# Which weight tiles are prepared ahead, and half of a stage's gates on GpSimd, in a top-k attention with two MLPs

## The chip, the cores and the metric

The kernel runs on one core of a Trainium2 chip. The metric is device microseconds of one execution, the median of several runs. The engines are named as the profile names them: PE (TensorE), DVE (VectorE), ACT (ScalarE), POOL (GpSimd), and SP, whose queue issues all transfers.

## The reference

Attention over q, k, v of 4 batches, 8 heads, 576 positions and 64 features, in which only the 32 largest scores of each row count; its output is 2304 tokens of 512 features. Two MLPs follow, each 512 to 2048 to 512:

```python
scores = scale * np.matmul(q, k.transpose(0, 1, 3, 2))
kth = np.partition(scores, -top_k, axis=-1)[..., -top_k:-top_k + 1]
attn = softmax(np.where(scores >= kth, scores, -1e9))      # top_k = 32
x = (attn @ v) as 2304 x 512
h = x @ w_in;  x = (h - np.tanh(h)) @ w_out                # first MLP
h = x @ w2_in; out = np.where(h > 0, h, np.exp(np.minimum(h, 0)) - 1) @ w2_out
```

## The kernel before

The 2304 tokens are worked on in six chunks of 384. A chunk's attention has four pairs of heads and eight groups (two per pair), each of three tiles of 128 query rows by 576 keys. For a tile, PE makes the scores (`ps`), ACT copies them to SBUF (`s`, line 385), and DVE finds the 32 largest: four times MAX8 (line 406) with three MATCH_REPLACE8 between (line 420). ACT or DVE makes the masked exponential (`e`), PE transposes it (`pt`), ACT copies that (`ph`), PE multiplies by v (`av`), and the result, times the reciprocal of the sum, is the chunk's `x`. The scores of groups 16 to 23 are computed early, in the time of the first chunk's attention, and parked in DRAM (`park`, lines 347 to 356).

A chunk's two MLPs (m = 0 and 1) go through 16 f-tiles of 128 hidden features each, numbered 0 to 31 over both. A step multiplies `x` with an f-tile's first matrix (`first`, line 577, 12 matmuls into PSUM tile `h`), forms the gate (`gate`), and multiplies with the second matrix into three PSUM banks (`second`, line 613, 9 matmuls). `first` and `gate` of the next step are issued ahead of `second` of this one. Products are done in three terms, of a high and a low part of each operand: ACT rounds to the high part and POOL subtracts it (`split`, lines 147 to 149). The gate of the first MLP is h - tanh(h): ACT makes the tanh (`t`, line 580), and DVE subtracts (line 596). In chunks where `GATE_GP` is k, the f-tiles with ft % 4 < k have ACT copy h to SBUF (line 593) and POOL subtract (line 594) instead. The gate of the second MLP is on ACT and DVE (lines 582, 583 and 591).

The weights come as raw 8-byte words. `prepare` (lines 177 to 213) loads one f-tile's raw words (1 MB, line 180), scales and converts them on ACT (lines 186 and 203), joins them on DVE (line 189), splits them on ACT and POOL into a tile of the ring `w` of six slots, and stores that to DRAM (line 213) for the later chunks, which load it from there (line 222). While the attention of the first chunk still goes on, scaling and joining are done in two halves through PSUM banks; the switch `wide` ends that when the last pair of the first chunk is transposed (line 445). The first chunk's MLPs use the prepared tile itself; but the f-tiles in `EARLY` are prepared in advance, from tick `PREP_AT` on and `PREP_RATE` ticks apart, only stored, and loaded later like those of other chunks (`load_next`, lines 215 to 222).

The order of the code is by ticks, four to a group. The first MLP of the first chunk begins at tick 36; six ticks before, `load_next` is called for f-tiles 0 to 5, one each tick, and then once behind each step's `second`, six f-tiles ahead. The last pair of the first chunk is handled at tick 32, behind that tick's `load_next`. This order is a priority: the framework's scheduler fixes each engine's own order when it builds the program, by these priorities, by which buffers are free, and by a timeline that it models. In the trace the first raw words are loaded at 7.6 us. Lines touched: 47 and 51.

Of the kernel before, what the change touches and what calls it, by code (L numbers as in the profile page):

```python
# [43 lines left out]

MASK_ACT = [3, 2, 1, 0, 0, 0]

GATE_GP = [0, 0, 1, 1, 1, 2]

EARLY = range(12, 21)
PREP_AT = 8
PREP_RATE = 2.5
AHEAD = 6
# [52 lines left out]
def tile_topk_attention_two_mlps(  # L107
# [64 lines left out]
    def weight_tile(name):  # L172
        return sb.tile([P, 2, 2, 512], F32R, tag="w", name=name, bufs=W2_BUFS)
# [3 lines left out]
    def prepare(m, ft):  # L177

        raw = sb.tile([P, 1024], I64, tag="wr", name=f"wr{m}_{ft}", bufs=RAW_BUFS)
        nc.sync.dma_start(raw, (w1, w2)[m][ft])  # L180
        words = raw.bitcast(F32).rearrange("p (n w) -> p n w", w=2)
        low, scaled = words.bitcast(U32)[:, :, 0], words[:, :, 1]
        w = sb.tile([P, 1024], F32, tag="wf", name=f"wf{m}_{ft}", bufs=WF_BUFS)

        def scale(out, src):
            nc.scalar.activation(out, src, AF.Prelu, scale=2.0**-112, alpha=-(2.0**32))  # L186

        def join(out, high, low):
            nc.vector.scalar_tensor_tensor(  # L189
                out.bitcast(U32), high.bitcast(U32), 3, low, op0=ALU.logical_shift_left, op1=ALU.bitwise_or  # L190
            )

        halves = [slice(0, 512), slice(512, 1024)]
        small = {}
        early = "wide" in stage
        if early:
            for a, cs in enumerate(halves):
                small[a] = bank(f"acc{stage['at'] % 3}", f"sc{m}_{ft}_{a}", 1)
                stage["at"] += 1
                scale(small[a], scaled[:, cs])  # L200
        else:
            scale(scaled, scaled)
        nc.scalar.activation(low.bitcast(I32), low, copy, scale=2.0**-29 * (1 - 2.0**-20), bias=-0.5 + 7.5 * 2.0**-20)
        if early:
            for a, cs in enumerate(halves):
                join(w[:, cs], small[a], low[:, cs])
        else:
            join(w, scaled, low)
        wt = weight_tile(f"wp{m}_{ft}")
        if m * NF + ft not in EARLY:  # L210
            weights[0, m, ft] = wt
        split(wt[:, :, 0], wt[:, :, 1], w.rearrange("p (h c) -> p h c", h=2))
        nc.sync.dma_start(f(scratch[m, ft]), f(wt))

    def load_next():
        if loads:
            ci, m, ft = loads.pop(0)
            if ci == 0 and m * NF + ft not in EARLY:
                prepare(m, ft)
# [366 lines left out]
    def gate(ci, m, ft):  # L586
# [3 lines left out]
        if m == 1:  # L590
            nc.vector.scalar_tensor_tensor(g, t, -1.0, h, op0=ALU.add, op1=ALU.max)  # L591
        elif ft % 4 < GATE_GP[ci]:
            nc.scalar.activation(g, h, copy)
# [135 lines left out]

    early = list(EARLY)  # L730
    for tick in range(FIRST_TICK, n_ticks):
        for do in before.get(tick, ()):
            do()
        while early and PREP_AT + PREP_RATE * (len(EARLY) - len(early)) <= tick:
            i = early.pop(0)
# [77 lines left out]
```

## Time and profile before

| | |
|---|---|
| median of 3 runs | 1222.76 us (1219.91 to 1224.75) |
| the profiled execution | 1219.57 us, span 1217.8 us |
| busy: PE, DVE, ACT, POOL | 1146.4, 944.5, 765.6, 497.9 us |
| mean granted clock of PE | 0.973 of full speed |
| raw weight loads (`wr`) | 32 of 1024 KB |
| stores of prepared tiles (`w<-wp`) | 32 of 1024 KB |
| loads of prepared tiles (`wt<-w`) | 169 of 1024 KB |

Busy times are sums over the whole span; the ends of matmuls are modelled, so PE's share is not a share of its peak. In the row of slices each digit is the busy share of one of 40 equal slices of 30.4 us, in tenths. A view of stages gives each engine's busy time between two times; a timeline gives single instructions, merged where alike; what stands in brackets behind one is how long its engine had been idle, and what ended that. A group `out<-in` names the tiles that an instruction writes and reads; `f32<-128x576` and the like are shapes.

### The profile page before, as it was taken

Reading aid. Unit: us, or ns where it says so; the run is one execution under the profiler, and the core shown is the slowest. Engines: PE = TensorE matmul, PEld = TensorE weight load, DVE = VectorE, ACT = ScalarE, POOL = GpSimd, SP = SyncE. Lnnn points to the kernel's source line nnn. Section 1 sums busy time; section 2 is a strip of 40 time slices with the busy share of each in tenths; the row PEclk is TensorE's granted clock in tenths of the full one; section 3 lists DMA queues with packets and bytes.
Section 4 is the critical chain, followed back from the end, with each engine's and each line's share of the span. In section 5 each row is a group of like instructions: output and inputs, shape, how many; then the busy total and the mean of one; then the engine's idle time right before and its main releaser. Section 6 shows DMA issues by size and latency. Waiting matters only on the chain.

```text
span 1217.8 us, 18856 instructions
## 1 busy us (share of the span) xinstructions
PE 1146.4 (94%) x6349; PEld 977.0 (80%) x6349; DVE 944.5 (78%) x1898; ACT 765.6 (63%) x1594; POOL 497.9 (41%) x557
## 2 busy tenths in 40 slices
PE   6577689999999999999999999999999999999998
PEld 3344368888888979898978988988998888898887
DVE  7999999998999999679987789898889995100111
ACT  5999987888984555565664566575655564432333
POOL 2445446657753313443423444444334422333222
PEclk9688889999999999999999999999999999999999
DMA  7999937985979986669986779978688645686572
GB/s 246 398 333 330 311 111 276 350 266 217 356 285 327 276 294 184 238 166 299 241 182 234 242 204 260 251 219 266 225 241 243 204 127 207 210 283 248 198 269 95
DMA packets 81616, 301.69 MB, mean 248 GB/s; under 512 B 18800, under 2 KB 36080, under 8 KB 51696
## 3 DMA queue, kind: packets, MB, share of 16 engines
q1 hardware_dynamic: 81520, 300.49, 76.5%
q8 instruction: 50, 0.82, 0.3%
q14 instruction: 46, 0.38, 0.1%
HBM read 255.07 MB, written 45.39 MB: 247 GB/s over the span
## 4 chain that ended last, share of the span: by engine, by line
PE 75%; ACT 6%; DVE 5%; DMA 3%; issue 1%; POOL 1%; another core or an unknown queue 0%; ACTq 0%; DVEq 0%; POOLq 0%
PE h L577 30%; PE acc L613 30%; PE av L470 6%; PE pt L448 5%; DMA wt<-w 3%; PE ps L383 2%; PE ps L384 2%; DVE vm L406 2%; DVE w L420 2%; DVE wf L189 1%; ACT ph L449 1%; ACT s L385 1%; ACT e L410 1%; ACT y L627 1%; ACT wr L186 0%
## 5 line engine op out<-in xcount | busy, mean ns | idle before, releaser
L149 POOL TENSOR_TENSOR gl<-g,gh 128x384 fp32r<-128x384 f32 x192 | 205.3, 1071 | 385.0 <-ACT gh L148 360.2
L406 DVE MAX8 vm<-w 128x8 f32<-128x576 f32 x432 | 315.0, 748 | 3.1
L613 PE MATMUL acc<-wt,gh 128*128 128x512 f32 x1014 | 270.9, 398 | 0.3 <-ACT gh L148 0.3
L613 PEld LDWEIGHTS acc<-wt,gh 128*128 128x128 f32 x1014 | 186.2, 188 | 34.9 <-issue 3.3
L420 DVE MATCH_REPLACE8 w<-vm,w 128x576 f32<-128x576 f32 x288 | 212.7, 740 | 0.0
L148 ACT ACTIVATE gh<-g 128x384 fp32r<-128x384 f32 x192 | 100.7, 525 | 81.2 <-DVE g L591 34.6
L613 PE MATMUL acc<-wt,gl 128*128 128x512 f32 x507 | 148.9, 398 | 1.0 <-POOL gl L149 1.0
L577 PE MATMUL h<-zh,wt 128*128 128x384 f32 (+2 forms) x776 | 146.4, 324 | 2.4 <-ACT zh L632 2.0
L591 DVE SCALAR_TENSOR_TENSOR g<-t,h 128x384 f32<-128x384 f32 x96 | 52.2, 544 | 124.2 <-ACT t L583 123.8
L406 DVE MAX8 vm<-s 128x8 f32<-128x576 f32 x144 | 107.2, 750 | 47.1 <-ACT s L385 44.4
L577 PE MATMUL h<-xh,wt 128*128 128x384 f32 x672 | 140.9, 339 | 1.2 <-DMA wt<-w 1.2
L385 ACT ACTIVATE s<-ps 128x288 f32<-128x288 f32 (+1 forms) x272 | 107.5, 418 | 48.3 <-PE ps L384 40.7
L449 ACT ACTIVATE ph<-pt 116x384 f32<-116x384 f32 (+1 forms) x240 | 111.5, 499 | 40.0 <-PE pt L448 37.4
L448 PE MATMUL pt<-ident,e 128*116 128x128 f32 (+1 forms) x720 | 115.2, 288 | 22.7 <-ACT e L423 9.9
L577 PEld LDWEIGHTS h<-zh,wt 128*128 128x128 f32 x776 | 125.8, 189 | 8.8 <-ACT zh L632 3.2
L448 PEld LDWEIGHTS pt<-ident,e 128*116 128x116 f32 (+1 forms) x720 | 90.0, 142 | 43.2 <-ACT e L423 12.6
L577 PEld LDWEIGHTS h<-xh,wt 128*128 128x128 f32 x672 | 117.4, 188 | 7.5 <-ACT t L580 1.0
L582 ACT ACTIVATE t<-h 128x384 f32<-128x384 f32 x96 | 46.8, 489 | 119.7 <-PE h L577 119.7
L613 PEld LDWEIGHTS acc<-wt,gl 128*128 128x128 f32 x507 | 93.3, 188 | 19.9 <-POOL gl L149 1.2
L420 DVE MATCH_REPLACE8 w<-vm,s 128x576 f32<-128x576 f32 x144 | 106.7, 741 | 0.0
L596 DVE TENSOR_TENSOR g<-h,t 128x384 f32<-128x384 f32 x76 | 41.4, 545 | 70.6 <-ACT t L580 69.9
L580 ACT ACTIVATE t<-h 128x384 f32<-128x384 f32 x96 | 47.2, 492 | 75.1 <-PE h L577 74.6
(82 smaller groups left out, 1938.7 us busy)
## 6 DMA issues: line engine op xcount, KB each, us to landing
wt<-w SPq DMA_DIRECT2D x169, 1024.0 KB, 6.5
wr<-in_w_dram SPq DMA_DIRECT2D x32, 1024.0 KB, 7.2
w<-wp SPq DMA_DIRECT2D x32, 1024.0 KB, 8.5
kraw<-in_kT_dram SPq DMA_DIRECT2D x96, 144.0 KB, 6.2
vraw<-in_vL_dram SPq DMA_DIRECT2D x64, 160.0 KB, 4.5
sd<-sp SPq DMA_DIRECT2D x24, 288.0 KB, 7.3
s<-sd SPq DMA_DIRECT2D x24, 288.0 KB, 9.0
qraw<-in_qT_dram SPq DMA_DIRECT2D x64, 96.0 KB, 5.7
```

The source lines that it names most:

```text
L148: nc.scalar.activation(hi, src, copy)
L149: return nc.gpsimd.tensor_sub(lo, src, f(hi))
L385: nc.scalar.activation(s[lo:hi, cs], pt[lo:hi, :HS], copy)
L406: nc.vector.max(g.vm[:, j, min(r, 1)], u.s[t] if r == 0 else g.w[j])
L420: nc.vector.match_replace(g.w[j], v, u.s[t] if r == 0 else g.w[j], FILL)
L448: nc.tensor.transpose(pt[:kn, j * P : j * P + P], v.e[t][:, k0 : k0 + kn], ident)
L449: nc.scalar.activation(g.ph[:kn, blk, :nq], pt[:kn, :nq], copy)
L470: nc.tensor.matmul(banks[c0][h * D : h * D + D, : v.n], v.vraw[h][:kn, blk], v.g.ph[:kn, blk, cs], start=(blk == order[0]), stop=(blk == o ...
L577: nc.tensor.matmul(h[:, cs], wv[:, wi, kt], xs[:, kt, cs], start=(a == 0), stop=(a == len(jobs) - 1))
L580: nc.scalar.activation(t, h, AF.Tanh)
L591: nc.vector.scalar_tensor_tensor(g, t, -1.0, h, op0=ALU.add, op1=ALU.max)
L613: nc.tensor.matmul(acc[ci, m][t], gx[:, t * P : t * P + P], wt[:, wi], start=(ft == 0 and k == 0), stop=(ft == NF - 1 and k == 2),)
```

## The change

Two constants change. `EARLY`, f-tiles 12 to 20 (nine of them), becomes 9, 12, 15, 18, 21, 24 and 27 (seven); the rest of `prepare` and `load_next` is as it was, so f-tiles 10, 11, 13, 14, 16, 17, 19 and 20 are prepared in the first chunk's MLPs or just before, as 22, 23, 25, 26 and 28 to 31 are, and 9, 21, 24 and 27 are loaded there. `GATE_GP` of the first chunk goes from 0 to 2: eight of its sixteen first-MLP gates (f-tiles 0, 1, 4, 5, 8, 9, 12, 13) take the way over lines 593 and 594.

```diff
-GATE_GP = [0, 0, 1, 1, 1, 2]
+GATE_GP = [2, 0, 1, 1, 1, 2]
...
-EARLY = range(12, 21)
+EARLY = [9, 12, 15, 18, 21, 24, 27]
 PREP_AT = 8
 PREP_RATE = 2.5
 AHEAD = 6
```

## Rows read from the trace of the kernel before

**Rows 1.** Page, part 2: PE's busy tenths in 40 slices.

```profile
...
PE   6577689999999999999999999999999999999998
...
```

**Rows 2.** Busy time by stage: PE, PEld, DVE, ACT, POOL, clock, DMA share, GB/s.

```profile
...
0.00:157.20 157.20, 107.08 (x392) 67.44 (x393) 144.60 (x285) 137.18 (x262) 64.53 (x86) 0.83 0.91 322
157.20:270.00 112.80, 105.56 (x625) 90.12 (x625) 107.05 (x208) 94.07 (x191) 65.68 (x69) 0.97 0.71 246
270.00:361.00 91.00, 88.64 (x572) 77.92 (x569) 87.83 (x164) 80.45 (x156) 62.27 (x61) 1.00 0.78 281
361.00:1070.00 709.00, 703.04 (x4042) 614.78 (x4041) 589.77 (x1219) 403.89 (x887) 263.81 (x302) 1.00 0.78 233
...
```

**Rows 3.** The same, finer.

```profile
...
157.20:215.00 57.80, 51.03 (x264) 42.83 (x263) 55.84 (x106) 47.10 (x95) 34.20 (x32) 0.94 0.54 182
215.00:270.00 55.00, 54.53 (x363) 47.30 (x363) 51.21 (x104) 46.97 (x97) 31.48 (x38) 1.00 0.90 314
...
300.00:330.00 30.00, 28.61 (x183) 24.70 (x182) 27.94 (x52) 29.03 (x54) 24.25 (x22) 1.00 1.00 366
...
```

**Rows 4.** Timeline of POOL, 332 to 361 us: start, us, instruction, idle before.

```profile
...
332.82 0.23 POOL L498 TENSOR_SCALAR r<-sum 128x3 f32<-128x3 f32 x1 [2.24 <-DVE e L427]
...
357.87 1.01 POOL L149 TENSOR_TENSOR xl<-xun,xh 128x384 fp32r<-128x384 f32 x1
...
```

**Rows 5.** Timeline of DVE, 157 to 177 us.

```profile
...
157.18 0.17 DVE L501 RECIPROCAL r<-r 128x6 f32<-128x6 f32 x1
...
```

**Rows 6.** Timeline of PE, 160.5 to 181.5 us.

```profile
...
160.77 0.62 PE L577 MATMUL h<-xh,wp 128*128 128x384 f32 x2 [2.24 <-ACT ph L449]
...
180.91 0.86 PE L613 MATMUL acc<-wp,gh 128*128 128x512 f32 x3
```

**Rows 7.** Tile wr: ns min/median/max, first and last start.

```profile
...
L203 ACT ACTIVATE wr<-wr x32: 1113/1144/1276, 16.2 to 347.4; 128x1024 int32<-128x1024 uint32 x32
L186 ACT ACTIVATE sc<-wr x24: 602/648/802, 14.8 to 98.1; 128x512 f32<-128x512 f32 x24
...
L186 ACT ACTIVATE wr<-wr x20: 1118/1154/1274, 107.8 to 346.4; 128x1024 f32<-128x1024 f32 x20
...
```

**Rows 8.** Tile wf.

```profile
...
L148 ACT ACTIVATE wp<-wf x32: 1040/1066/1225, 21.9 to 351.3; 128x1024 fp32r<-128x1024 f32 x32
L149 POOL TENSOR_TENSOR wp<-wf,wp x32: 2355/2390/3398, 23.1 to 355.1; 128x1024 fp32r<-128x1024 f32 x32
...
L189 DVE SCALAR_TENSOR_TENSOR wf<-wr x20: 1195/1216/3120, 110.5 to 349.2; 128x1024 uint32<-128x1024 uint32 x20
...
```

**Rows 9.** Groups by line on DVE, 0 to 157.2 us: busy, mean ns, idle before.

```profile
...
L406 DVE MAX8 vm<-s 128x8 f32<-128x576 f32 x25 | 18.8, 750 | 8.2 <-ACT s L385 8.1
...
L189 DVE SCALAR_TENSOR_TENSOR wf<-sc,wr 128x512 uint32<-128x512 uint32 x24 | 15.8, 681 | 2.5 <-ACT wr L203 2.1 <-issue 0.4
L189 DVE SCALAR_TENSOR_TENSOR wf<-wr 128x1024 uint32<-128x1024 uint32 x5 | 7.2, 1430 | 1.5 <-issue 1.5
...
```

**Rows 10.** Instructions on tile wp by stage: PE, PEld, ACT, POOL.

```profile
...
0.00:157.20 157.20, 0.00 (x0) 0.00 (x0) 16.32 (x15) 35.50 (x15) 0.83 0.91 322
157.20:270.00 112.80, 57.02 (x252) 46.12 (x252) 7.46 (x7) 16.79 (x7) 0.97 0.71 246
270.00:361.00 91.00, 46.10 (x213) 37.15 (x213) 10.66 (x10) 25.67 (x11) 1.00 0.78 281
...
```

**Rows 11.** Tile g.

```profile
...
L596 DVE TENSOR_TENSOR g<-h,t x76: 529/544/559, 175.9 to 1135.9; 128x384 f32<-128x384 f32 x76
L593 ACT ACTIVATE g<-h x20: 484/486/525, 533.7 to 1129.4; 128x384 f32<-128x384 f32 x20
L594 POOL TENSOR_TENSOR g<-g,t x20: 1006/1015/1027, 534.5 to 1130.0; 128x384 f32<-128x384 f32 x20
...
```

**Rows 12.** Timeline of all engines, 188 to 189 us.

```profile
...
188.40 2.39 POOL L149 TENSOR_TENSOR wp<-wf,wp 128x1024 fp32r<-128x1024 f32 x1
...
188.83 3.03 DVE L189 SCALAR_TENSOR_TENSOR wf<-wr 128x1024 uint32<-128x1024 uint32 x1
...
```

## The prediction

> **What bounds the kernel now.** I read the page first: PE's row of slices stands at 5 to 8 tenths in the first six and at 9 from the seventh on [rows 1]. So the span has two parts. Then I cut the span into stages [rows 2]. Up to 157.2 us DVE is busy 144.60 us and ACT 137.18, while PE is a filler: this is the opening, the first chunk's attention, bound by DVE with ACT close behind. From 157.2 to 270 (the first chunk's first MLP) and from 270 to 361 (its second) DVE is still near full, but PE is full too; from 361 to 1070 PE is busy 703.04 of 709 us and DVE 589.77. The part after 1070 is PE alone.
>
> That PE is the later bound is seen in its idle time: 6.77 us in 157.2 to 215, 0.47 in 215 to 270, 1.39 in 300 to 330 [rows 3]. And DVE's fullness before 361 is mostly work done ahead: the last normalizer of the second chunk is computed at 332.82 and its last x only at 357.87 [rows 4], so attention could slip by some 20 us before the second chunk's MLP at 361 waits for it. The end is therefore the start of the first MLP plus PE's work plus PE's idle time behind it. The change acts on the first and the third.
>
> What sets the start: DVE finishes the last pair's normalizer at 157.18, the first matmul of the MLP is at 160.77 and the first of the second layer at 180.91 [rows 5, 6].
>
> **The change part by part.**
>
> *Two preparations fewer in the opening.* A preparation is two ACT scalings of half a tile (0.648 us each) and one ACT conversion (1.144), DVE's join (two halves of 0.681, or one of 1.216), an ACT copy (1.066) and a POOL subtraction (2.390) [rows 7, 8]. Before: 24 half joins and 5 whole ones lie before 157.2 us, which is 17 tiles [rows 9], of which 15 are also split [rows 10]: nine early tiles, f-tiles 0 to 5, and two more that are joined and wait for a slot, since six slots hold f-tiles 0 to 5 until the MLP uses them. After: seven, six and two, 15 tiles joined. The switch from half joins to whole ones falls behind the third of f-tiles 0 to 5 in the code, so four half joins go and the five whole ones stay: DVE loses 4 x 0.681 = 2.7 us. DVE has no cover here, so the start moves by this. From below: 0, if DVE takes top-k steps of the next chunk in its place; from above: ACT loses 2 x (2 x 0.648 + 1.144 + 1.066) = 7.0 us, and if ACT were the true bound of the opening the start would move by all of it. Of DVE's idle time in the opening, 2.5 + 1.5 us stand before joins and end with ACT's conversions or with issue [rows 9]; with ACT 7.0 us lighter I take half of that, 2.0 us. Sum: -4.7, with 0 and -7.0 as ends. The DMAs that go with them (for each early tile 1 MB read, 1 MB stored, and later 1 MB loaded; the non-early ones are stored too, so of two tiles only the loads vanish) cost nothing: the stores and reads move from the opening, where DMA is at 0.91, to a stage at 0.71 [rows 2].
>
> *Four more preparations in the first MLP, two fewer in the second.* Tiles are split six ahead of their use. From 157.2 to 270 ACT splits 7 tiles, f-tiles 6 to 11 and 21, because 12 to 20 are loads; from 270 to 361 ten, 22 to 31 [rows 10]. After the change the first stretch splits 6, 7, 8, 10, 11, 13, 14, 16, 17, 19 and 20, eleven, and the second 22, 23, 25, 26 and 28 to 31, eight. ACT gains 4 x (1.154 + 1.144 + 1.066) = 13.5 us in the first [rows 7, 8] and, with the gates below, goes from 94.07 to 111.5 of 112.8 us. What ACT then has late is partly attention, which has its 20 us; partly it is copies that PE waits for. Bounds for PE's added idle time: 0, since PE loses 0.47 us in 215 to 270 with ACT at 46.97 of 55; and 6.0, if that stretch lost as much as 157.2 to 215 does now (6.77 of 57.8 us). The nearest row is 300 to 330, where ACT is at 29.03 of 30 and PE loses 1.39 [rows 3]: for 55 us that is 2.5, less the 0.5 that is there, +2.0. In the second MLP ACT gets 2 x 3.364 = 6.7 us lighter; the 1.39 us of 300 to 330 may halve, -0.7 (ends 0 and -1.4). DVE's joins there and here are covered by its lead.
>
> *Half of the first gates on POOL.* In f-tiles 0, 1, 4, 5, 8, 9, 12 and 13 of the first MLP, DVE's subtraction (0.544) becomes an ACT copy (0.486) and a POOL subtraction (1.015) [rows 11]. DVE loses 8 x 0.544 = 4.4 us, which only adds to its lead; ACT gains 3.9, counted above; POOL gains 8.1, and with 4 x 2.39 for splits goes from 65.68 to 83.4 of 112.8 us. Once the pipeline runs, a gate is a step ahead of its use, so I cost six of the eight at nothing; what hides them is the first layer of the next f-tile on PE, and if that cover fails each costs its extra 0.486 + 1.015 - 0.544 = 0.96 us. The first two stand in the filling of the pipeline, between the first matmul of the first layer and the first of the second, 20 us later [rows 6]. One of them is on the path: +1.0. From below -0.5, since two MAX8 of 0.75 us [rows 9] can stand ahead of a gate in DVE's full queue while POOL is free; from above +3.4, if a 2.39 us split stands ahead of it on POOL.
>
> [...] DVE's whole joins take 1.195 us at least and up to 3.120 [rows 8]; one of 3.03 starts at 188.83, while a POOL split of 188.40 runs for 2.39 [rows 12]. [...]
>
> **Sum.** -4.7 + 2.0 - 0.7 + 1.0 = -2.4 us. The profiled execution took 1219.57 us (span 1217.8 and 1.8 around it), so it would take 1217.2. It lies 3.2 us under the median of the runs shown, 1222.76; from the median the same step gives 1220.4, which is my forecast.
>
> **Rivals.**
>
> 1. ACT was the opening's bound. For it: ACT is at 137.18 of 157.2, its work there cannot be put off, and DVE's longest waits are for ACT's s copies, 8.1 us [rows 9], most of it the start of the program. Against: DVE's idle time behind the start is below 6 us, so more than 2.7 plus that cannot come. Then -7.0 for the opening, none of the +2.0, -0.7, +0.5: -7.2, 1215.6.
>
> 2. ACT becomes the bound of the first MLP. For it: 111.5 of 112.8. Against: attention's lead. ACT idles 18.7 us of that stretch now, waiting for PE and DVE; if it goes on needing these waits, the stretch lasts 111.5 + 18.7 = 130.2, 17.4 longer; less 4.7 and 0.7 this is +12.0, 1234.8. It decides once more than 10.8 of the 17.4 us reach PE (there the change passes +0.5%).
>
> 3. [...] Eight gates at 0.96 us each, 7.7, and four more joins stretched from 1.2 to 3.03 us, 7.3, with the second layer waiting for POOL's gl behind each: 15.0 if all reach PE, less 5.4: +9.6, 1232.4. It decides from 11.5 of the 15. Against: DVE's lead covers the joins.
>
> 4. The opening does not shorten: the 2.7 us that DVE gets are filled with the next chunk's top-k, which lies interleaved there. Then only +2.3 is left: 1225.1.
>
> **How the numbers follow.** Forecast 0.42, rivals 0.29, 0.11, 0.06 and 0.12. The measurement of this kernel can tell about 0.5% (6.1 us) from no change. Faster than 1216.6: most of rival 1 (0.24) and the low side of the forecast (0.08), 0.32. Slower than 1228.9: rivals 2 and 3 (0.14), a little of the forecast and of 4 (0.03), 0.17. Same: 0.51. The forecast's own terms span -7.0 + 0 - 1.4 - 0.5 = -8.9 to 0 + 6.0 + 0 + 3.4 = +9.4; both ends together are unlikely, so 1214 to 1227 would be its own range. For all cases I go from 1212, which holds rival 1, to 1231, which leaves out rivals 2 and 3 and a low tail, some 0.2 in all.
>
> **What would show it.** Opening: 20 half joins instead of 24, the first L577 matmul at 155 to 158 us (rival 4: at 160 to 161; rival 1: at 153 to 154). First MLP: ACT above 95% from there on for 110 us and PE's idle time in it 2 to 4 us more; if PE's idle time grows by over 10, rival 2 or 3 is on, and who PE waits for tells them apart (ACT's ph, s and gh, or POOL's gl). Joins: a mean above 2 us beside POOL's gates speaks for 3. Gates: the first L613 matmul 20 to 22 us behind the first L577. Wrong altogether would be the forecast if the difference arose behind 361 us, where the change alters nothing: then the order that the scheduler gives the instructions has moved, and the sum above has no term for that.

## The result, and the profile after

The changed kernel takes 1228.73 us (median of 7 runs, 1225.81 to 1233.40), the kernel before 1222.03 beside it (7 runs, 1219.40 to 1224.75). The ratio is 1.0064 [1.0044, 1.0084]: 0.6% slower, where I forecast 1220.4 and no change or a small gain. The profiled execution took 1227.15 us, its span 1225.4, 7.6 more than before.

The page after: PE's tenths and its granted clock in 40 slices.

```profile
...
PE   6577799989899999999999999999999999999998
...
PEclk9689899989999999999999999999999999999999
...
```

The dips at the ninth and eleventh slice (245 to 276 and 306 to 337 us) are new against [rows 1]. Next the stages of [rows 2], after (busy time and number of instructions of PE, PEld, DVE, ACT and POOL, then clock, DMA share and GB/s; PEld is PE's weight loads, LDWEIGHTS in the trace):

```profile
...
0.00:157.20 157.20, 110.84 (x428) 68.97 (x430) 146.86 (x294) 138.18 (x270) 64.10 (x86) 0.86 0.83 298
157.20:270.00 112.80, 103.08 (x601) 89.82 (x597) 111.11 (x191) 99.30 (x192) 85.99 (x79) 0.95 0.83 292
270.00:361.00 91.00, 85.24 (x537) 73.67 (x534) 85.03 (x154) 74.49 (x146) 54.29 (x53) 0.96 0.79 274
361.00:1070.00 709.00, 701.77 (x4031) 613.67 (x4030) 592.90 (x1222) 401.22 (x885) 261.27 (x306) 1.00 0.77 227
...
```

PE does 428 matmuls in the opening instead of 392, and then 601 instead of 625 and 537 instead of 572: it comes out of the opening ahead and reaches 361 us behind. In the second stage DVE goes from 107.05 to 111.11 of 112.8, ACT only from 94.07 to 99.30. The finer windows of [rows 3]:

```profile
...
157.20:215.00 57.80, 53.93 (x307) 46.89 (x303) 57.80 (x103) 49.70 (x100) 44.56 (x43) 1.00 0.69 241
215.00:270.00 55.00, 49.16 (x298) 42.93 (x295) 53.31 (x89) 49.60 (x93) 41.42 (x37) 0.91 0.97 346
300.00:330.00 30.00, 29.34 (x185) 24.18 (x184) 27.99 (x49) 26.78 (x51) 24.38 (x19) 1.00 0.87 307
...
```

DVE is busy for all of the first 57.80 us. PE's idle time, 6.77, 0.47 and 1.39 us before, is 3.87, 5.84 and 0.66.

**How far ahead.** PE does the same 6349 matmuls in every kernel here. I weigh each matmul with its usual spacing (0.234 us for 128x512, 0.174 for 128x384, and so on) and ask when a kernel has done as much as the kernel before has done at time t. That time minus t is its position: negative is ahead. Beside it stands the start of the first chunk's last gate (the sixteenth of line 591 on DVE), and in the last columns the gaps over 1 us between matmul starts from 195 to 1100 us, and the time at half the granted clock there. Each row is the one profiled execution of a kernel; n4's took 1245.13 us, 4.9 more than its median, the others lie within 3 us of theirs.

| kernel | at 200 | 361 | 500 | 1000 | end of span | last gate | gaps: us | half clock, us |
|---|---|---|---|---|---|---|---|---|
| before | 0 | 0 | 0 | 0 | 0 | 364.5 | 5: 7.9 | 6.8 |
| after | -13.9 | +4.3 | +11.2 | +8.1 | +7.6 | 365.1 | 7: 15.3 | 23.9 |
| e1 tiles only | -7.0 | +3.5 | +9.2 | +5.4 | +4.9 | 364.3 | 7: 14.3 | 10.2 |
| e2 gates only | -4.2 | +5.6 | +5.1 | +1.6 | +1.0 | 368.7 | 6: 9.1 | 0 |
| e3 | -8.4 | +0.2 | +8.7 | +4.9 | +4.5 | 367.2 | 6: 10.1 | 6.8 |
| e4 | -1.5 | +7.4 | +11.9 | +9.3 | +8.7 | 369.1 | 7: 11.8 | 13.7 |
| n2 | +1.1 | +8.8 | +15.4 | +14.3 | +14.2 | 372.4 | 8: 16.3 | 13.7 |
| n3 | +1.4 | +1.6 | +2.2 | +2.4 | +1.7 | 366.1 | 5: 8.5 | 3.4 |
| p before | +0.3 | +7.2 | +13.4 | +9.9 | +9.3 | 369.3 | 4: 10.3 | 10.2 |
| p after | -7.0 | +0.2 | +9.8 | +7.5 | +7.0 | 361.9 | 7: 12.5 | 17.1 |
| a1 | -13.6 | +4.5 | +12.4 | +10.5 | +10.0 | 365.2 | 11: 19.9 | 23.9 |
| a2 | -11.8 | +2.2 | +7.5 | +4.0 | +3.5 | 364.8 | 6: 11.1 | 13.7 |
| a3 | -11.5 | -1.5 | -0.5 | -3.3 | -3.8 | 360.5 | 4: 7.9 | 6.8 |
| n4 | +3.8 | +12.7 | +24.3 | +24.4 | +25.6 | 375.1 | 12: 25.2 | 17.1 |
| d1 | -11.5 | +9.2 | +21.2 | +18.2 | +17.8 | 371.9 | 18: 28.8 | 17.1 |
| d2 | -10.4 | +0.8 | +6.8 | +4.5 | +4.0 | 357.0 | 12: 17.6 | 10.2 |
| d5 | -10.2 | +5.5 | +4.6 | +2.3 | +1.8 | 367.1 | 9: 15.7 | 6.8 |
| d6 | +3.4 | +26.2 | +33.8 | +31.6 | +31.3 | 387.7 | 12: 23.1 | 23.9 |
| f1 | -3.1 | +14.3 | +23.1 | +23.0 | +23.2 | 376.1 | 11: 22.1 | 23.9 |
| f2 | -12.1 | -3.5 | -2.3 | -5.6 | -6.1 | 358.6 | 4: 7.9 | 3.4 |

After is 13.9 us ahead at 200 us, loses 18.2 by 361 and 6.9 more by 500, and gets 3 to 4 back. Those two losses are what has to be explained.

### The profile page after: what moved, and what is told of

Same layout as the page of the kernel before. It is cut to its first block, busy times and chain, and to the rows that moved or that the text cites. A ratio compares the mean times of both kernels' runs of the same rounds, so it can differ in the third digit from the quotient of the medians.

```text
span 1225.4 us, 18857 instructions
## 1 busy us (share of the span) xinstructions
PE 1150.5 (94%) x6349; PEld 979.6 (80%) x6349; DVE 952.8 (78%) x1888; ACT 766.8 (63%) x1600; POOL 509.6 (42%) x565
## 4 chain that ended last, share of the span: by engine, by line
PE 59%; ACT 3%; DVE 2%; DMA 1%; POOL 0%; issue 0%; ACTq 0%; POOLq 0%; DVEq 0%
PE acc L613 25%; PE h L577 24%; PE av L470 4%; PE pt L448 3%; PE ps L383 2%; PE ps L384 2%; DMA s<-sd 1%; DVE vm L406 1%; DVE w L420 1%; ACT y L627 1%; ACT e L410 1%; ACT ph L449 0%; ACT zh L632 0%; ACT s L385 0%; POOL kk L149 0%
## 5 line engine op out<-in xcount | busy, mean ns | idle before, releaser
L613 PE MATMUL acc<-wt,gh 128*128 128x512 f32 x1002 | 268.9, 399 | 3.1 <-ACT gh L148 3.1
L613 PEld LDWEIGHTS acc<-wt,gh 128*128 128x128 f32 x1002 | 184.6, 189 | 37.8 <-ACT gh L148 4.6
L613 PE MATMUL acc<-wt,gl 128*128 128x512 f32 x501 | 146.9, 398 | 0.0
L577 PE MATMUL h<-zh,wt 128*128 128x384 f32 (+2 forms) x752 | 143.6, 326 | 1.6 <-ACT zh L632 1.2
L577 PE MATMUL h<-xh,wt 128*128 128x384 f32 x664 | 141.0, 341 | 3.2 <-DVE g L596 2.3
L577 PEld LDWEIGHTS h<-zh,wt 128*128 128x128 f32 x752 | 122.7, 188 | 8.7 <-ACT zh L632 2.1
L577 PEld LDWEIGHTS h<-xh,wt 128*128 128x128 f32 x664 | 117.0, 189 | 11.1 <-DVE g L596 2.5
L613 PEld LDWEIGHTS acc<-wt,gl 128*128 128x128 f32 x501 | 92.3, 189 | 18.2
L427 DVE SCALAR_TENSOR_TENSOR e<-s,vm,e 128x576 f32<-128x576 f32 x99 | 96.8, 982 | 2.0 <-ACT e L410 1.1
```

The costliest lines, as they stand in the source:

```text
L427: nc.vector.scalar_tensor_tensor(u.e[t], u.s[t], v[:, 7:8], u.e[t], op0=ALU.is_ge, op1=ALU.mult, accum_out=g.sum[:, j : j + 1])
L577: nc.tensor.matmul(h[:, cs], wv[:, wi, kt], xs[:, kt, cs], start=(a == 0), stop=(a == len(jobs) - 1))
L613: nc.tensor.matmul(acc[ci, m][t], gx[:, t * P : t * P + P], wt[:, wi], start=(ft == 0 and k == 0), stop=(ft == NF - 1 and k == 2),)
```

## The experiments

The theories were: the new number and place of the preparations cost it (A; A1 is their place, A2 their number); the gates on GpSimd do (B); the order that the scheduler lays on each engine is another one, and the kernel before happens to have one that fits (C); DVE alone is the bound up to the last gate (D); DVE's joins and masked exponentials take longer beside POOL's subtractions, as the join of 3.03 us at 188.83 in [rows 12] did, and this costs the time (P). Each ratio is against the kernel before, timed beside it; that kernel's medians lie between 1216.70 and 1222.03.

**e1_tiles_only and e2_gates_only: each part by itself.**

```diff
-EARLY = range(12, 21)
+EARLY = [9, 12, 15, 18, 21, 24, 27]
```

> The new EARLY list alone, first gates all on DVE as before. Theory A (the eleven preparations in the first MLP, in place of seven, load ACT, DVE and POOL there, attention falls behind and PE idles): nearly the whole loss stays, 1226 to 1230 us, second MLP layer's start near 171 us as with both edits. [...]

```diff
-GATE_GP = [0, 0, 1, 1, 1, 2]
+GATE_GP = [2, 0, 1, 1, 1, 2]
```

> Eight first gates on POOL alone, nine early tiles 12 to 20 as before. Theory A: within 3 us of the kernel before, 1219 to 1225, the opening unchanged (first L577 matmul near 161 us). Theory B: slower by more than the two edits together, since no shorter opening pays for it: 1232 to 1240.

e1: 1224.21 us against 1216.70, 1.0063 [1.0040, 1.0086]. e2: 1220.34, 1.0021 [1.0005, 1.0037]. The tiles alone give the whole loss; but they are also 7.0 us ahead at 200, and the gates alone 4.2: at the start both parts gain, and with both it is 13.9. The loss comes later in both, by 10.5 and 9.8 us up to 361.

**e3_seven_in_row and e4_nine_spread: number against place.**

```diff
-EARLY = range(12, 21)
+EARLY = range(12, 19)
```

> Seven early tiles in a row, 12 to 18, gates as before: two preparations fewer in the opening, and the two come in the second MLP (f-tiles 19 and 20), not in the first. Theory A1 (it is the place of the preparations, four more in the first MLP, that costs): faster than before, 1213 to 1219, opening shorter by 5 to 10 us and kept. Theory A2 (it is their number, 25 in the MLPs for 23): about as slow as the new list alone, 1226 to 1230.

```diff
-EARLY = range(12, 21)
+EARLY = range(9, 27, 2)
```

> Nine early tiles, every second one from 9 to 25, gates as before: as many preparations in the opening as before, but about three more in the first MLP and three fewer in the second. Theory A1: slower than before with no gain of the opening, 1228 to 1236. Theory A2: as before, 1220 to 1225.

e3: 1225.68, 1.0077 [1.0053, 1.0102]; e4: 1228.27, 1.0097 [1.0067, 1.0127]. Fewer in the same place loses as much as the change, and as many in other places loses more. Neither number nor place is the cause by itself, which put theory C first.

**n2_row_from_11, n4_row_from_13, n3_prep_at_9: the order alone.** The same nine preparations, one f-tile number earlier, one later, or the same numbers one tick later.

```diff
-EARLY = range(12, 21)
+EARLY = range(11, 20)
```

> The kernel before with its nine early tiles one number lower, 11 to 19: the same count of preparations in the opening, in the first MLP (f-tiles 6 to 10, 20 and 21: seven) and in the second. A control for the order alone, since the scheduler lays the engines' orders anew. [...] Theory C (the loss comes from any new order, because the order of before happens to fit what the engines really take): slower by 4 to 12 us.

```diff
-EARLY = range(12, 21)
+EARLY = range(13, 22)
```

> The kernel before with its nine early tiles one number higher, 13 to 21. Third control for the order. Theory C: slower than before by 4 to 14 us as the row from 11 is. If the row from 11 was slow by its numbers (fewer f-tiles prepared ahead of the turn between the MLPs), the row from 13 would be the same as before or faster.

```diff
-PREP_AT = 8
+PREP_AT = 9
```

> The kernel before with PREP_AT 9 instead of 8: the early preparations one tick later, nothing else. Second control. Theories A and B: within 3 us of before. Theory C: slower by 2 to 10 us, with idle time of PE behind 200 us that before does not have.

n2: 1233.41 against 1221.18, 1.0109 [1.0083, 1.0135]. n4: 1240.19 against 1220.41, 1.0156 [1.0115, 1.0196]. n3: 1221.51, 1.0003 [0.9988, 1.0017]. Moving the row by one f-tile number changes the place of one preparation and not their count, and has no price in the sum; yet it costs 1.7 to 2.4 times the change's whole loss, in either direction. The same numbers one tick later cost nothing.

**p_before_memset and p_after_memset: theory P.** POOL's subtraction for the weights (2.390 us, [rows 8]) becomes two memsets of the low part (0.96 us each), so the weights' low part is left out. Once on the kernel before, once on the one after.

```diff
-        split(wt[:, :, 0], wt[:, :, 1], w.rearrange("p (h c) -> p h c", h=2))
+        nc.scalar.activation(wt[:, :, 0], w.rearrange("p (h c) -> p h c", h=2), copy)
+        nc.gpsimd.memset(f(wt[:, :, 1]), 0.0)
+        nc.gpsimd.memset(f(wt[:, :, 1]), 0.0)
```

> The kernel before, but POOL's subtraction of the prepared weights' low part is left out, two POOL memsets in its place (the low part is zero, so part of the arithmetic is left out): POOL stays about as long at work, but reads nothing from SBUF. [...] If the order decides (theory C), the time can be on either side.

> Both edits with the same replacement. Theory P: faster than the kernel with both edits by 8 us or more, and at or below the same replacement without the edits, 1208 to 1216, since the opening gains 10 us and nothing takes it back. Theory A (ACT and the number of preparations): it stays 4 to 8 us slower than the replacement without the edits.

p_before: 1229.50 against 1221.18, 1.0078 [1.0054, 1.0101]. p_after: 1226.60, 1.0056 [1.0037, 1.0075]. The whole joins, 157.2 to 361 us (DVE by line and form: busy, mean ns, idle before); p_before, p_after:

```profile
...
L189 DVE SCALAR_TENSOR_TENSOR wf<-wr 128x1024 uint32<-128x1024 uint32 x15 | 20.2, 1349 | 4.7 <-ACT wr L203 4.3 <-ACT wp L212 0.4
...
```

```profile
...
L189 DVE SCALAR_TENSOR_TENSOR wf<-wr 128x1024 uint32<-128x1024 uint32 x17 | 21.1, 1242 | 5.5 <-ACT wr L203 5.4
...
```

and the last gates of the two (DVE's timeline; the lines lie two lower here):

```profile
...
369.32 0.54 DVE L593 SCALAR_TENSOR_TENSOR g<-t,h 128x384 f32<-128x384 f32 x1
...
```

```profile
...
361.92 0.54 DVE L593 SCALAR_TENSOR_TENSOR g<-t,h 128x384 f32<-128x384 f32 x1
...
```

With the memsets the joins, at means of 1.349 and 1.242 us, are near the 1.2 us that they take at least [rows 8]; with the subtraction, up to the last gate, the means were 1.557 and 1.715. The change then brings the last gate 7.4 us earlier, where with the subtraction it brings it 0.6 later. But a new order alone moves this gate as far (n2 by 7.9 us, n4 by 10.6), so the two runs show that the joins are shorter without the subtraction, and not what its presence costs. The times don't show it either: p_after did not come down to the 1208 to 1216 us of theory P, the two ratios' intervals overlap, and p_before itself lost 8.3 us though it has less to do.

**a1_rate_3_5, a2_third_from_10, a3_quarter_gates: neighbours of the change.** On the kernel after: the preparations further apart in time, every third from 10 on, or four gates on GpSimd instead of eight.

```diff
-PREP_RATE = 2.5
+PREP_RATE = 3.5
```

> Both edits, the seven early preparations spread over the ticks that nine took before (PREP_RATE 3.5): a small new order on the side of the change. Theory C (the order decides, by where PE meets gaps of 2 us and more and then the half clock): if its gaps stay where they are, 1225 to 1232. Theory A (number and place of the preparations): the same as both edits within 3 us.

```diff
-EARLY = [9, 12, 15, 18, 21, 24, 27]
+EARLY = [10, 13, 16, 19, 22, 25, 28]
```

> Both edits with the list one number higher, 10 to 28: the same seven tiles by count, a new order. Theory C: anywhere from 1212 to 1236, with PE's gaps and half-clock time at other places and the time following their sum. Theory A: within 3 us of both edits, 1224 to 1232.

```diff
-GATE_GP = [2, 0, 1, 1, 1, 2]
+GATE_GP = [1, 0, 1, 1, 1, 2]
```

> Both edits with four of the sixteen first gates on POOL instead of eight. Theory B (the gates): between the list alone and both edits. Theory C: no such ordering; time follows its own gaps, 1212 to 1236.

a1: 1229.58 against 1220.41, 1.0061 [1.0038, 1.0084]. a2: 1222.26, 1.0008 [0.9991, 1.0025]. a3: 1214.44, 0.9949 [0.9927, 0.9972]. Four gates fewer on GpSimd turn the loss into a gain; one f-tile number takes most of it away.

**f1_quarter_gates_only and f2_quarter_rate_3_5: is a3 a rule?** Its gates on the kernel before, and its edits with a1's rate.

```diff
-GATE_GP = [0, 0, 1, 1, 1, 2]
+GATE_GP = [1, 0, 1, 1, 1, 2]
```

> Four first gates on POOL, the nine early tiles 12 to 20 as before. If four gates are what is good: 1212 to 1218. If the order decides: 1218 to 1236, as with most new orders.

```diff
-GATE_GP = [0, 0, 1, 1, 1, 2]
+GATE_GP = [1, 0, 1, 1, 1, 2]
...
-EARLY = range(12, 21)
+EARLY = [9, 12, 15, 18, 21, 24, 27]
 PREP_AT = 8
-PREP_RATE = 2.5
+PREP_RATE = 3.5
```

> Four first gates on POOL and seven early tiles as in the fastest run, with PREP_RATE 3.5. A small new order; with eight gates it changed nothing. It should stay faster than before, 1211 to 1218, if the fastest run's margin is not a single order's luck.

f1: 1242.61 against 1221.34, 1.0181 [1.0145, 1.0217]. f2: 1215.36, 0.9955 [0.9938, 0.9972]. Four gates alone lose 1.8% and eight alone 0.2%, while with the seven tiles four gain 0.5% and eight lose 0.6%: the two parts have no prices that add up.

**d5_quarter_from_10, d1_both_masks_on_act, d2_quarter_masks_on_act, d6_before_masks_on_act: is DVE the bound?** d5 is a3 with a2's f-tiles. The others take the second chunk's masked exponentials that DVE still had, one of three in each group, and give them to ACT: d1 in the kernel after, d2 in a3, d6 in the kernel before. The first diff is d5 against the kernel after, the second the edit of d1, d2 and d6.

```diff
-GATE_GP = [2, 0, 1, 1, 1, 2]
+GATE_GP = [1, 0, 1, 1, 1, 2]
...
-EARLY = [9, 12, 15, 18, 21, 24, 27]
+EARLY = [10, 13, 16, 19, 22, 25, 28]
```

> Four gates on POOL with the seven early tiles one number higher, 10 to 28: does the gain of four gates hold under a neighbouring order? If the number of gates is what counts: 1212 to 1218. If the order decides (theory C): anywhere from 1212 to 1236.

```diff
-MASK_ACT = [3, 2, 1, 0, 0, 0]
+MASK_ACT = [3, 3, 1, 0, 0, 0]
```

> Both edits, and the third of three masked exponentials of each group of the second chunk on ACT instead of DVE. Theory D (DVE is the bound up to the first chunk's last gate, 365.1 us with both edits, and its two-input operations beside POOL make it so): that gate 5 to 12 us earlier, the time 4 to 12 us below both edits, 1215 to 1224. Theory A (ACT): the gate later, the time 1230 to 1238.

> Four gates on POOL, seven early tiles, and the same masks on ACT. Theory D: the gate at 352 to 358 us for 360.5, the time 1206 to 1213. Theory A: 1216 to 1224.

> The kernel before with the same masks on ACT. Theory D: its first chunk's last gate earlier than 364.5 us by 4 to 10, the time 1212 to 1219. Theory C (any new order loses what before has by its fitting one): 1222 to 1234.

d5: 1220.62 against 1221.71, 0.9990 [0.9975, 1.0006]. d1: 1235.93, 1.0113 [1.0091, 1.0136]. d2: 1223.46, 1.0018 [0.9999, 1.0038]. d6: 1248.10, 1.0220 [1.0198, 1.0241]. All three with less DVE work are slower than their bases. DVE's longest wait from 157.2 us to the last gate (us in total, times, longest), d6:

```profile
...
DVE vm L406 <- ACT s L385: 14.4, 5, 5.4
...
```

and before:

```profile
...
DVE vm L406 <- ACT s L385: 5.4, 6, 2.2
...
```

Theory D falls as far as the times go: in d6 DVE waits 9.0 us longer for ACT's copies of the scores. In d2 the gate did come 3.5 us earlier than in a3, as D had it, and the end still came 7.8 later. And a3's gain is gone one f-tile number on (d5).

## Why the prediction was wrong, point by point

**The opening: right in its mechanism, too small by half.** The first matmul of the MLP and the first of its second layer, after (PE's timeline, to be read beside [rows 6]):

```profile
...
150.94 0.62 PE L577 MATMUL h<-xh,wp 128*128 128x384 f32 x2
...
170.68 1.17 PE L613 MATMUL acc<-wp,gh 128*128 128x512 f32 x4
...
```

Both come 10 us earlier, where the term was -4.7 and its end -7.0. DVE's last normalizer of the first chunk, after, against 157.18 before [rows 5]:

```profile
...
149.88 0.16 DVE L501 RECIPROCAL r<-r 128x6 f32<-128x6 f32 x1
...
```

Of the 9.8 us up to the first L577 matmul, 7.3 come before this normalizer: DVE spends 2.3 less on half joins, 1.1 less on whole ones, 1.3 less on top-k, and is idle 2.5 less. The other 2.5 come behind it, where the sum took the way to the first matmul as fixed: it was 3.59 us, with PE's wait of 2.24 for ACT's ph in it [rows 6], and is 1.06. The joins up to 157.2 us are as forecast, 20 half and 5 whole (compare [rows 9]), with 13, 11 and 8 splits in the three stages (compare [rows 10]); the idle time before the joins falls by 1.4 of the 2.0 us that I took:

```profile
...
L189 DVE SCALAR_TENSOR_TENSOR wf<-sc,wr 128x512 uint32<-128x512 uint32 x20 | 13.1, 682 | 2.0 <-ACT wr L203 1.7 <-issue 0.2
L189 DVE SCALAR_TENSOR_TENSOR wf<-wr 128x1024 uint32<-128x1024 uint32 x5 | 6.1, 1215 | 0.6 <-POOL nk L412 0.6
...
```

```profile
...
0.00:157.20 157.20, 2.35 (x12) 2.04 (x12) 14.85 (x13) 30.78 (x13) 0.86 0.83 298
157.20:270.00 112.80, 65.74 (x306) 52.35 (x306) 11.71 (x11) 26.86 (x11) 0.95 0.83 292
270.00:361.00 91.00, 45.32 (x197) 36.16 (x198) 8.44 (x8) 19.22 (x8) 0.96 0.79 274
...
```

The start moves with the tiles alone: the first L577 matmul is at 152.91 in e1 and at 160.79 in e2. The gates, charged at +1.0, gave time all the same: the first L613 matmul comes 24.89 us behind the first L577 in e1, where DVE makes these gates, and 19.74 after.

**The failed step: PE's time behind the start, which the sum has at +2.0 and -0.7.** These terms rest on three steps: "DVE's fullness before 361 is mostly work done ahead"; a small price for the copies on ACT that PE waits for; and an end that is "the start of the first MLP plus PE's work plus PE's idle time behind it", with PE's work a fixed sum. The same 1002 matmuls take 161.0 us before, from 200 on, and 179.2 after, from 186.1 on (columns as in [rows 2]):

```profile
...
200.00:361.00 161.00, 157.64 (x1002) 138.32 (x1002) 154.04 (x297) 142.25 (x280) 101.17 (x104) 0.99 0.84 298
...
186.10:365.30 179.20, 164.86 (x1002) 143.10 (x1001) 171.02 (x301) 151.25 (x287) 121.57 (x118) 0.95 0.86 305
...
```

Of the 18.2 us, 11.0 are PE's idle time (3.36 and 14.34) and 7.2 are the matmuls themselves (157.64 and 164.86), at a lower mean clock (0.99 and 0.95). So two terms that came to +1.3 measured +18.2. Whom PE waited for in these stretches (us in total, times, longest), the longest before:

```profile
...
PE pt L448 <- ACT s L385: 1.3, 3, 0.5
PE acc L613 <- POOL gl L149: 1.0, 1, 1.0
...
```

and after:

```profile
...
PE h L577 <- DVE g L591: 3.9, 1, 3.9
PE ps L383 <- ACT s L385: 3.1, 3, 2.0
PE yt L630 <- ACT y L627: 1.5, 1, 1.5
PE h L577 <- ACT zh L632: 1.4, 1, 1.4
...
```

In all, ACT ended 9.6 us of these waits (before 2.1), DVE 4.6 (0.3) and POOL none (1.0).

*ACT's copies, the term +2.0.* From 215 to 270 us PE's idle time rose by 5.4 us, from 0.47 to 5.84, close to the term's bound of 6.0, and every wait in it ended with ACT. Rival 2 had ACT full there; it was busy 99.30 of 112.8 us in the first MLP, where I forecast 111.5. But in seven of the waits between 186.1 and 365.3 us, 5.3 us together, the awaited copy or exponential stands on ACT right behind an instruction of a preparation. One of them, ACT's timeline after (PE had finished the input of `zh` at 258.1):

```profile
...
258.08 1.17 ACT L186 ACTIVATE wr<-wr 128x1024 f32<-128x1024 f32 x1
259.14 1.11 ACT L203 ACTIVATE wr<-wr 128x1024 int32<-128x1024 uint32 x1
260.28 1.57 ACT L632 ACTIVATE zh<-yt 128x512 fp32r<-128x512 f32 x3
...
```

PE's:

```profile
...
261.41 0.79 PE L577 MATMUL h<-zh,wp 128*128 128x256 f32 x2 [1.39 <-ACT zh L632]
...
```

*DVE's lead.* In the second MLP, where I forecast -0.7, PE's idle time rose by 3.4 us (2.36 to 5.76 from 270 to 361), and DVE's gate alone took 3.89 of it. The gates stand in one fixed row with the other chunks' top-k: 365 to 389 MAX8 and MATCH_REPLACE8 come before the first chunk's last gate on DVE. That gate, before:

```profile
...
364.50 0.53 DVE L591 SCALAR_TENSOR_TENSOR g<-t,h 128x384 f32<-128x384 f32 x1
...
```

after:

```profile
...
365.06 0.55 DVE L591 SCALAR_TENSOR_TENSOR g<-t,h 128x384 f32<-128x384 f32 x1 [0.52 <-ACT t L583]
...
```

and a3:

```profile
...
360.53 0.56 DVE L591 SCALAR_TENSOR_TENSOR g<-t,h 128x384 f32<-128x384 f32 x1 [0.47 <-ACT t L583]
...
```

The 10 us at the start are gone at this gate. DVE's account up to it, before against after: top-k 268.2 and 266.9 us, gates 14.3 and 10.8, idle 21.5 and 18.5; on the other side joins 43.3 and 45.4, masked exponentials 13.6 and 18.5, others 3.6 and 4.9. What is saved (7.8) is given back (8.3). That this row is what holds the last gate is not shown: after and in a3 DVE stood idle just before it, waiting for ACT's t.

**Rival 3, which I put at 0.06, took part.** DVE by line and form from 157.2 us to the last gate, before:

```profile
...
L189 DVE SCALAR_TENSOR_TENSOR wf<-wr 128x1024 uint32<-128x1024 uint32 x15 | 23.4, 1557 | 0.7 <-ACT wr L203 0.6
...
L427 DVE SCALAR_TENSOR_TENSOR e<-s,vm,e 128x576 f32<-128x576 f32 x11 | 11.3, 1030 | 0.2
...
```

and after:

```profile
...
L189 DVE SCALAR_TENSOR_TENSOR wf<-wr 128x1024 uint32<-128x1024 uint32 x17 | 29.2, 1715 | 0.5 <-POOL wp L149 0.5
...
L427 DVE SCALAR_TENSOR_TENSOR e<-s,vm,e 128x576 f32<-128x576 f32 x10 | 16.1, 1607 | 0.3
...
```

Two joins more, and both kinds longer. Against free lengths of 1.2 us (join) and 0.8 (masked exponential), which are near the least that each took before (1.195 in [rows 8], and 0.790), DVE lost 7.7 us before and 16.6 after, most of it (5.4 and 12.2) beside POOL's subtraction for the weights. I argued "DVE's lead covers the joins", and did not price the masked exponentials at all. The other half of this rival did not come: none of the long ones ended behind one of the new gates on POOL, PE's matmuls did not wait for POOL's gl, and the mean of the joins stayed below the 2 us that I had named as the rival's sign. At one place the loss can be followed to PE. DVE's timeline after (start, us):

```profile
...
328.76 3.42 DVE L189 SCALAR_TENSOR_TENSOR wf<-wr 128x1024 uint32<-128x1024 uint32 x1
...
333.50 2.87 DVE L427 SCALAR_TENSOR_TENSOR e<-s,vm,e 128x576 f32<-128x576 f32 x1
...
337.76 0.54 DVE L591 SCALAR_TENSOR_TENSOR g<-t,h 128x384 f32<-128x384 f32 x1
...
```

POOL's:

```profile
...
328.70 2.41 POOL L149 TENSOR_TENSOR wp<-wf,wp 128x1024 fp32r<-128x1024 f32 x1
...
333.41 2.35 POOL L149 TENSOR_TENSOR wp<-wf,wp 128x1024 fp32r<-128x1024 f32 x1 [0.19 <-ACT wp L148]
...
```

PE's:

```profile
...
330.47 1.55 PE L577 MATMUL h<-zh,wt 128*128 128x384 f32 x8
...
338.35 2.93 PE L577 MATMUL h<-zh,wp 128*128 128x384 f32 x8 [3.89 <-DVE g L591]
...
```

The join ends at 332.18: POOL's split ends at 331.11, and a free join takes 1.2. The exponential ends at 336.37: 335.76 and a free 0.8. So each ends one free length behind the end of the split that it met, within 0.2 us. Why it does is not shown. The gate stands behind both, which took 4.3 us over their free lengths, and PE idles 3.89 us for it. How much of the loss at the end is due to these long instructions is not shown.

**PE's clock took a part.** The granted clock is 0.50 of full (0.51 by the last window) in four stretches from 190 to 1100 us (windows after):

```profile
...
254.30:264.50 10.20, 7.83 (x35) 7.42 (x36) 10.03 (x20) 10.07 (x19) 4.04 (x3) 0.50 0.95 368
336.20:343.00 6.80, 4.65 (x16) 4.54 (x17) 6.80 (x17) 2.44 (x6) 1.24 (x2) 0.50 0.75 286
404.50:407.90 3.40, 3.40 (x12) 3.40 (x11) 3.40 (x9) 2.63 (x7) 1.59 (x4) 0.50 0.47 159
452.20:455.60 3.40, 3.40 (x11) 2.62 (x11) 3.40 (x9) 1.45 (x5) 0.81 (x1) 0.51 0.45 181
...
```

Before has one up to 500 us:

```profile
...
199.50:202.90 3.40, 3.13 (x10) 2.79 (x10) 3.40 (x9) 3.40 (x5) 1.98 (x2) 0.51 1.05 341
...
```

The stretch at 336.20 holds the 3.89 us wait, and the same eight matmuls take 2.93 us in it instead of 1.55. Taken as half speed, and those eight matmuls took 1.9 times as long, 23.8 us do the work of 11.9: an estimate of up to 11.9 us against 1.7, where PE is what the others wait for. The sum has no term for this.

**"Wrong altogether … if the difference arose behind 361 us": a part did.** The change alters nothing there, and 6.9 us are lost up to 500. PE's work of that stretch, before and after:

```profile
...
361.00:500.00 139.00, 137.56 (x773) 118.62 (x772) 132.37 (x284) 76.45 (x163) 42.61 (x65) 1.00 0.85 269
...
365.30:511.20 145.90, 140.84 (x774) 121.38 (x773) 135.21 (x288) 75.31 (x164) 39.65 (x63) 0.98 0.79 235
...
```

Idle time is 3.6 us of it, and slower matmuls 3.3. DVE's waits from 361 to 480, after:

```profile
...
DVE vm L406 <- DMA s<-sd: 9.6, 4, 3.7
...
```

before:

```profile
...
DVE vm L406 <- DMA s<-sd: 2.4, 1, 2.4
...
```

The parked scores come back late four times instead of once. In a3 it is once, 3.9 us, and a3 loses only 1.0 us in this stretch. What delays them was not tried by itself.

**What decides the sign.** Moving nine unchanged preparations by one f-tile number costs 1.1 or 1.6%, and four gates cost +1.8% or bring -0.5% by what else is set. So the direct prices in my sum, none over 5 us, are smaller than what another fixed order does (up to 19.8 us in n4, by the medians), and the kernel before is one of the well-fitting orders. Which property of an order makes it fit stays open: neither the last gate's time nor the position at 361 tells the end by itself (e1's gate is 0.2 us earlier than before, its end 4.9 later; d2's 7.5 earlier, its end 4.0 later). More buffers for `s`, which might loosen the order, were not tried.

**A better version came out.** a3, the change with four gates instead of eight, is faster than both: 0.9949 [0.9927, 0.9972]. f2, which also spaces the preparations by 3.5 ticks, repeats it: 0.9955 [0.9938, 0.9972]. With the f-tiles one number higher (d5) the gain is gone: 0.9990 [0.9975, 1.0006].

**Luck, and two slips.** That the measured time lies between 1212 and 1231 us is luck: the opening gained 5 us more than its term, and the stretch behind it lost 17 more than its terms. Two sums among the rivals are wrong, without changing the forecast. Rival 1's terms come to -7.0 and 1215.8 us, not -7.2 and 1215.6, and the term that it calls +0.5 is +1.0 in the sum; rival 2 passes +0.5% from 11.5 of its 17.4 us on, as rival 3 does, not from 10.8.

## What to carry to other kernels

An early start is worth only what the engines that feed PE can keep up with. Before adding a gain at the start to the end, ask for each engine that PE waits for what stands ahead of the awaited copy or gate in its fixed order, and how long that takes beside the other engines; an engine with idle time left can still be late, as ACT here, which was busy 151.25 of 179.20 us and ended 9.6 us of PE's waits. Where a scheduler fixes the order, run one or two edits with no price of their own (an index moved by one) beside the change: their spread, here 1 to 1.6%, is the least that a cause must exceed. Tune such constants together, since their effects don't add up.

## What the runs showed of the hardware that was not expected

After, DVE's joins and masked exponentials that met POOL subtractions took up to 3.42 us (a join, where the median before is 1.216, [rows 8]) and 2.94 (a masked exponential, where it is 0.808), while two POOL memsets in the place of the weights' subtraction left the joins at a mean of 1.24 to 1.35. After, 16 of them between 157.2 us and the last gate took over 0.15 us longer than free, and each ended 0.11 to 0.19 us less than its free length behind the end of a POOL instruction.

Some waits of PE inside a busy stage were followed by matmuls at half the granted clock: eight of line 577 took 2.93 us behind the wait of 3.89, and 1.55 at the full clock. After, single waits of 3.89, 2.28 and 2.31 us go over into 6.8, 3.4 and 3.4 us at half the granted clock; before, one of 2.24 goes over into 3.4. It is no fixed rule: a wait of 1.99 us (after, up to 194.18) has no half clock behind it, and the 10.2 us from 254.30 on come with shorter waits, of 0.45, 0.70, 1.47 and 1.39 us between 251 and 262 us.
